# First row tile of tokens in one transfer, and 16 lines of a bias loaded first from ScalarE

## The chip, the cores and the metric

The kernel runs on one core of one Trainium2 chip. The metric is the device time of one execution in microseconds. Each engine of the core (PE for matmuls, with its weight loads as PEld; VectorE, called DVE; ScalarE, called ACT; GpSimd, called POOL; SyncE, called SP) runs its own list of instructions in order, and waits on semaphores for the others and for transfers.

## The reference, cut to what matters

```python
def _A_ref(x, wqkv, wo):                      # x 1 x 2048 x 448, 16 heads of 28
    qkv = (x @ wqkv).reshape(B, S, 3, H, Dh).transpose(2, 0, 3, 1, 4)
    q, k, v = qkv
    idx = pos[:, None] - arange(8) * 2        # eight earlier positions, two apart
    logits = einsum("bhsd,bhswd->bhsw", q, k[idx]) * Dh ** -0.5
    attn = softmax(where(idx >= 0, logits, -1e9))
    return einsum("bhsw,bhswd->bhsd", attn, v[idx]).reshape(B, S, D) @ wo

def _B_ref(x, w1, b1, w2, b2):                # hidden width 1792
    h = relu(x @ w1 + b1)
    return (h * h) @ w2 + b2

g = sigmoid((x * gate_w).sum(-1, keepdims=True))
out = g * _A_ref(x, wqkv, wo) + (1 - g) * _B_ref(x, w1, b1, w2, b2)
```

All data are float32.

## The kernel before

Every matmul is done in three products of a reduced float32 type: each operand is split into a high part (a cast on ScalarE, or on VectorE) and a low part (the difference, on VectorE), and high times high, high times low and low times high are summed in PSUM. The 2048 tokens are four column blocks `c` of 512, held transposed: `xT[c]` has 128 partitions, and 4 row tiles `k` of the width 448, three of 128 rows and a last one of 64 rows that stands twice. "First row tile of tokens" is `xT[0, :, 0]`: 128 lines of 512 numbers, 256 KB.

The program first multiplies all four blocks with the weights of q, k and v (`qkv`), then runs the hidden layer (`h`, `b`) with the attention on GpSimd and VectorE beside it, and last the projection (`a`). A planner written in Python lays out the order of each engine's instructions: it keeps a clock of PE's work, and `when(t, ...)` and `at(dt, ...)` put a load or a split into the program when that clock comes to `t`.

The opening is written out by hand. PE runs 13 warm-up matmuls on a tile of zeros (line 634, tile `zero`, line 631). SP issues for each `k` a transfer of the weights of q (`raws[0]`, `wqraw` in the profile) and then the tokens (`rx`, `xraw`); for `k` = 0 the tokens come in two transfers of 256 columns. Each is split as soon as it is there: line 657 makes the weights' high part on ScalarE, lines 662 and 664 the tokens' high part in two halves of 256 columns (for the very first half on VectorE, line 662), lines 665 and 667 the low parts on VectorE:

```python
        for i, cols in enumerate(halves):
            if k == i == 0:
                nc.vector.tensor_copy(x.h[k][:, cols], rx[:, k, cols])
            else:
                nc.scalar.activation(x.h[k][:, cols], rx[:, k, cols], AF.Copy)
```

`qkv_first` (line 255) then does the first 36 matmuls, 12 for each of three row tiles: for `k` = 0 first those of token groups 0 and 1 (columns 0 to 255), then those of groups 2 and 3. The matmuls of the fourth row tile and all later ones are issued in pairs on the two halves of PE's rows (line 186).

`b1z` is a small tile: columns 0 to 13 hold the first bias (`b1t`, 128 lines of 14 numbers, 56 bytes), and one number in column 15 of partition 0 is a zero (`none`, set in line 632). `biases()` loads `b1` and `b2` from SP when the planner's clock is at 70 us. All loads are issued by SP. The load of the tokens of block 1 (`x_load`, line 561) is four transfers, one for each row tile.

Of the kernel before, what the change touches and what calls it, by code (L numbers as in the profile page):

```python
# [14 lines left out]
P = 128  # L15
# [7 lines left out]
CH = 512  # L23
# [34 lines left out]
def gated_mix_kernel(ctx: ExitStack, tc: tile.TileContext, xT, wqkv, w1, w2, wo, b1, b2, out):  # L58
    nc = tc.nc
# [43 lines left out]
    b1t, none = b1z[:, :NF], b1z[0:1, 15:16]  # L103

    ctx.enter_context(tc.manual_schedule())
    nc.gpsimd.memset(mask, 0.0)
    for s in range(HALO):
        nc.gpsimd.memset(mask[0:1, s, 0:HALO - s], -1e9)
# [388 lines left out]
    def raw_tile(name):  # L497
        return rawp.tile([P, 4, 512], F32, tag="raw", name=name)
# [62 lines left out]
    def x_load(c):  # L561
        raw = raw_tile(f"xraw{c}")
        if c == 1:
            for k in range(4):
                nc.sync.dma_start(raw[:, k, :CH], xT[c, :, k])
        else:
            nc.sync.dma_start(raw[:, :, :CH], xT[c])
        return raw
# [69 lines left out]
    rx = raw_tile("xraw0")  # L638
    for k in range(4):
        if k < 3:  # L640
            nc.sync.dma_start(raws[0][:, k, :NQ], wqkv[0, :, k])
        else:
            for b, rows in ((0, slice(0, 64)), (1, slice(64, P))):
                nc.sync.dma_start(raws[0][rows, k, :NQ], wqkv[b, rows, k])
        for cols in ((slice(0, 256), slice(256, CH)) if k == 0 else (slice(0, CH),)):
            nc.sync.dma_start(rx[:, k, cols], xT[0, :, k, cols])

    for b, tag in ((1, "k"), (2, "v")):
        raw = attp.tile([P, 3, D], F32, tag=tag, name=f"wqraw{b}")
# [67 lines left out]

    xs, xm = {0: x}, {}
    xraw = {1: x_load(1)}
    SPLIT_AT = {1: 19000.0, 2: 35000.0, 3: 53500.0}  # L720

# [16 lines left out]
    def x_more(c):  # L738
        xraw[c] = x_load(c)
# [3 lines left out]
            nc.sync.dma_start(d.rearrange("a g r c -> (a g) r c")[:, 0:HALO], halo0)  # L743

    def biases():
        nc.sync.dma_start(b1t, b1)
        nc.sync.dma_start(b2t, b2.partition_broadcast(P))

    for k in range(3):
# [22 lines left out]
    when(67000.0, w1_piece, 2, 77400.0, 1450.0)  # L772
    when(68000.0, w1_piece, 3, 83300.0, 1450.0)
    when(70000.0, biases)
    when(86000.0, w2_piece, 0, 4, 93000.0, 1400.0)
    when(89600.0, w2_piece, 4, 3, 100200.0, 1400.0)
# [312 lines left out]
    c, x = ORDER[0], xm[3]  # L1089
# [8 lines left out]
    for g in range(2, 2 * NF):  # L1098
        i, f = g // (NF // 2), g % (NF // 2) * 2
        c = ORDER[i]  # L1100
# [120 lines left out]
```

## Time and profile before

| | us |
|---|---|
| median of 3 runs | 413.23 (413.23 to 413.26) |
| profiled execution | 413.8 |
| its span | 412.0 |
| PE busy | 407.8 (99%) |
| DVE busy | 270.6 (66%) |
| POOL busy | 268.4 (65%) |
| ACT busy | 210.4 (51%) |

The profile is of one execution. Its span counts from the first instruction of the program to the last; the rest of its own time lies around it. In the views, a row of the timeline gives the start and the length in us, the engine, the line of the kernel, the operation, the tile written and the tiles read, the shape, and how many; in brackets stands how long the engine was idle before it, and what ended that. SPq is the queue that issues transfers: the length of its row is the time of issuing, not of the transfer. In the rows of busy time by stretch stand the stretch, its length, the busy time of PE, PEld, DVE, ACT and POOL with the instructions in it, the clock granted to PE, the share of the DMA engines, and GB/s.

### The profile page before, as it was taken

The page shows a single profiled execution, that of the slowest core. Times are in us where ns is not written, and L with a number is a line of the kernel's source. Part 1 is how long each engine was busy: PE and PEld are TensorE (multiplying, and loading weights), DVE is VectorE, ACT ScalarE, POOL GpSimd, SP SyncE. Part 2 cuts the span into 40 slices and gives each one's busy share as a digit, 9 for nine tenths or more (in the row PEclk, how much of TensorE's full clock was granted, in tenths as well). Part 3 has the DMA queues.
Part 4 walks back from the last instruction along what each step waited for, and adds up shares of the span by engine and source line. Part 5 has one row for each costly group of instructions (what it writes and reads, how often), then busy time and mean ns, then how long its engine had stood idle before and what let it go on. Part 6 is the DMA issues. An engine that isn't in the chain of part 4 may idle for free.

```text
span 412.0 us, 9331 instructions
## 1 busy us (share of the span) xinstructions
PE 407.8 (99%) x3835; PEld 366.0 (89%) x3835; DVE 270.6 (66%) x430; ACT 210.4 (51%) x461; POOL 268.4 (65%) x167
## 2 busy tenths in 40 slices
PE   8999999999999999999999999999999999999997
PEld 7999999999888888888888888989898888888996
DVE  4590745276767766787656798879576677892354
ACT  4641646387775555444565535444653254346540
POOL 0000001955999999989989899999899977940000
PEclk9999999999999999999999999999999999999999
DMA  7999999979262315654112649765146530168304
GB/s 213 368 351 309 286 390 288 355 223 315 91 241 99 128 51 209 208 186 152 41 47 105 222 158 270 196 146 154 28 157 200 217 130 2 45 179 132 95 0 181
DMA packets 66763, 73.83 MB, mean 179 GB/s; under 512 B 33120, under 2 KB 59296, under 8 KB 66464
## 3 DMA queue, kind: packets, MB, share of 16 engines
q1 hardware_dynamic: 66720, 73.23, 55.4%
q8 instruction: 30, 0.49, 0.5%
q14 instruction: 13, 0.11, 0.1%
HBM read 45.74 MB, written 28.28 MB: 180 GB/s over the span
## 4 chain that ended last, share of the span: by engine, by line
PE 99%; DVE 0%; issue 0%
PE b L186 33%; PE h L186 32%; PE qkv L186 23%; PE a L186 7%; PE qkv L255 2%; PE warm L634 1%; PE a L993 1%; PE last L993 0%; DVE bt L872 0%; PE last L985 0%; PE a L985 0%; DVE zero L631 0%; DVE b1z L632 0%
## 5 line engine op out<-in xcount | busy, mean ns | idle before, releaser
L335 POOL TENSOR_TENSOR qk<-q,k 128x896 f32<-128x896 f32 x64 | 135.2, 2144 | 84.2 <-DMA k<-k_d 76.0
L342 POOL TENSOR_TENSOR av<-lg,v 128x896 f32<-128x896 f32 x64 | 119.2, 1957 | 6.2 <-DVE lg L336 5.6
L621 DVE TENSOR_TENSOR h<-h,h 128x512 fp32r<-128x512 f32 x56 | 38.4, 688 | 66.8 <-ACT h L624 66.5
L186 PE MATMUL qkv<-wqh,x 64*128 64x448 f32 x528 | 78.2, 359 | 0.0
L336 DVE TENSOR_REDUCE lg<-qk 128x32 f32<-128x896 f32 x64 | 67.0, 1074 | 0.0
L350 DVE TENSOR_REDUCE o<-av 128x112 f32<-128x896 f32 x64 | 66.4, 1070 | 0.1
L186 PE MATMUL b<-w2ah,h 64*128 64x448 f32 x448 | 66.3, 359 | 0.0
L186 PE MATMUL b<-w2bh,h 64*128 64x448 f32 x448 | 66.1, 359 | 0.0
L622 ACT ACTIVATE h<-h,b1z 128x512 f32<-128x512 f32 x56 | 36.7, 655 | 43.6 <-PE h L186 43.6
L186 PEld LDWEIGHTS qkv<-wqh,x 64*128 64x128 f32 x528 | 49.4, 184 | 3.6
L186 PE MATMUL qkv<-wql,x 64*128 64x448 f32 x264 | 47.7, 358 | 0.0
L186 PEld LDWEIGHTS b<-w2bh,h 64*128 64x128 f32 x448 | 42.1, 184 | 3.5
L186 PEld LDWEIGHTS b<-w2ah,h 64*128 64x128 f32 x448 | 42.0, 184 | 3.7
L205 ACT ACTIVATE st<-qkv 128x448 f32<-128x448 f32 x48 | 23.5, 542 | 34.3 <-PE qkv L186 31.7
L186 PE MATMUL b<-w2bl,h 64*128 64x448 f32 x224 | 40.7, 358 | 0.0
L186 PE MATMUL b<-w2al,h 64*128 64x448 f32 x224 | 40.5, 358 | 0.0
L623 ACT ACTIVATE h<-h 128x512 fp32r<-128x512 f32 x56 | 33.5, 598 | 1.7
L624 ACT ACTIVATE h<-h 128x512 f32<-128x512 f32 x56 | 33.3, 594 | 0.0
L573 ACT ACTIVATE h<-h 128x4 fp32r<-128x4 f32 (+1 forms) x35 | 7.2, 207 | 44.4 <-PE b L186 44.2
L186 PE MATMUL h<-x2b,w1h 64*128 64x512 f32 x168 | 28.1, 386 | 0.0
L186 PE MATMUL h<-x,w1h 64*128 64x512 f32 x168 | 28.1, 386 | 0.0
L186 PE MATMUL h<-x1b,w1h 64*128 64x512 f32 x168 | 28.1, 386 | 0.0
(150 smaller groups left out, 688.6 us busy)
## 6 DMA issues: line engine op xcount, KB each, us to landing
k<-k_d SPq DMA_DIRECT2D x8, 840.0 KB, 5.6
v<-v_d SPq DMA_DIRECT2D x8, 840.0 KB, 5.0
x_d<-x SPq DMA_DIRECT2D x11, 512.0 KB, 6.8
q_d<-st SPq DMA_DIRECT2D x8, 448.0 KB, 5.5
k_d<-st SPq DMA_DIRECT2D x8, 448.0 KB, 5.2
v_d<-st SPq DMA_DIRECT2D x8, 448.0 KB, 5.8
w1raw<-w SPq DMA_DIRECT2D x4, 896.0 KB, 9.2
q<-q_d SPq DMA_DIRECT2D x8, 448.0 KB, 3.6
```

Source lines behind the costliest of these rows:

```text
L186: nc.tensor.matmul(acc.pt[:, :acc.n], a[rows], w[rows], start=acc.todo == acc.all, stop=acc.todo == 1)
L205: nc.scalar.activation(st[:, :, t % 2], pt[:, :D].rearrange("p (g c) -> p g c", g=G), AF.Copy)
L255: nc.tensor.matmul(acc.pt[:, :D], a, w, start=k == j == 0, stop=False)
L335: nc.gpsimd.tensor_mul(pr, q[:, s:s + 1].to_broadcast([P, W, C]), k[:, s:s + W])
L336: pending.append(lambda: nc.vector.tensor_reduce(lg[:, s], pr.rearrange("p w (h d) -> p w h d", h=HG), axis=AX.X, op=ALU.add))
L342: nc.gpsimd.tensor_mul(pr.rearrange("p (h d) w -> p w h d", h=HG), lg[:, s][:, :, :, None].to_broadcast([P, W, HG, DH]), v[:, s:s + W].rea ...
L350: nc.vector.tensor_reduce(o[:, g * C:(g + 1) * C], pr, axis=AX.X, op=ALU.add)
L573: nc.scalar.activation(ap, f32(ap), AF.Copy)
L621: nc.vector.tensor_sub(hl, pt, f32(hh))
L622: ops += [lambda pt=pt, r=r: nc.scalar.activation(pt, pt, AF.Relu, bias=b1t[:, f + r:f + r + 1]), lambda pt=pt, hh=hh: nc.scalar.activatio ...
L623: lambda pt=pt, hh=hh: nc.scalar.activation(hh, pt, AF.Square),
L624: lambda pt=pt, r=r, low=low: (nc.scalar.activation(pt, pt, AF.Square), at(delays[r], low))]
```

## The change

ScalarE issues, as its first instruction, the transfer of lines 0 to 15 of the first bias; the later load from SP brings lines 16 to 127. The tokens of block 0, row tile 0, come in one transfer of 512 columns instead of two of 256; their splits stay in halves. In `x_load` the four transfers of block 1 are written with slices of length one and are the same transfers.

```diff
     ctx.enter_context(tc.manual_schedule())
+    nc.scalar.dma_start(b1t[0:16], b1[0:16])
     nc.gpsimd.memset(mask, 0.0)
...
         if c == 1:
-            for k in range(4):
-                nc.sync.dma_start(raw[:, k, :CH], xT[c, :, k])
+            for ks in [slice(k, k + 1) for k in range(4)]:
+                nc.sync.dma_start(raw[:, ks, :CH], xT[c, :, ks])
...
-        for cols in ((slice(0, 256), slice(256, CH)) if k == 0 else (slice(0, CH),)):
-            nc.sync.dma_start(rx[:, k, cols], xT[0, :, k, cols])
+        nc.sync.dma_start(rx[:, k], xT[0, :, k])
...
     def biases():
-        nc.sync.dma_start(b1t, b1)
+        nc.sync.dma_start(b1t[16:P], b1[16:P])
         nc.sync.dma_start(b2t, b2.partition_broadcast(P))
```

## The prediction

> **What bounds the kernel now.** I read the page first, then the chain of waits, then the timeline of the first 14 us, because the change touches only what is loaded there.
>
> ```profile
> span 412.0 us, 9331 instructions
> PE 407.8 (99%) x3835; PEld 366.0 (89%) x3835; DVE 270.6 (66%) x430; ACT 210.4 (51%) x461; POOL 268.4 (65%) x167
> ...
> PE 99%; DVE 0%; issue 0%
> ```
> ```profile
> 4.34 8.87 PE qkv L255 x36
> 13.21 91.55 PE qkv L186 x912
> 104.76 2.77 PE h L186 x24
> ```
>
> PE is busy 99% of the span and carries 99% of the chain. The second fence is the chain in order of time (start, length, what). The 912 matmuls from 13.21 run as pairs on two row halves, 456 pairs in 91.55 us, 0.2 us a pair. There is no hole in that, so what shifts the start of this stream shifts the end by as much: nothing later can absorb it. The question is the 36 matmuls of line 255 before it, which need the first row tile of tokens. The timeline of their stretch (start, length, engine, line, what; in brackets the idle time before it and what ended it):
>
> ```profile
> 0.74 1.28 ACT L657 ACT_TABLE_LOAD   x1 [0.74 <-PEq L1213]
> 0.75 0.39 SPq L641 DMA_DIRECT2D wqraw<-wqkv  x1
> 1.08 0.06 DVE L632 MEMSET b1z<- 1x1 f32 x1
> 1.19 3.14 PE L634 MATMUL warm<-zero 128*128 128x256 f32 x13 [1.19 <-DVE b1z L632]
> 1.19 0.89 SPq L646 DMA_DIRECT2D xraw<-xT  x2
> 2.13 0.43 SPq L641 DMA_DIRECT2D wqraw<-wqkv  x1
> 2.60 0.43 SPq L646 DMA_DIRECT2D xraw<-xT  x1
> 3.45 0.58 ACT L657 ACTIVATE wqh<-wqraw 128x448 fp32r<-128x448 f32 x1 [1.43 <-DMA wqraw<-wqkv]
> 3.79 0.29 DVE L662 CAST x<-xraw 128x256 fp32r<-128x256 f32 x1 [2.65 <-DMA xraw<-xT]
> 4.06 0.62 DVE L665 TENSOR_TENSOR wql<-wqraw,wqh 128x448 fp32r<-128x448 f32 x1
> 4.22 1.09 PE L255 MATMUL qkv<-wqh,x 128*128 128x448 f32 x2
> 5.62 0.42 ACT L664 ACTIVATE x<-xraw 128x256 fp32r<-128x256 f32 x1 [1.59 <-DMA xraw<-xT]
> 7.66 0.72 ACT L664 ACTIVATE x<-xraw 128x256 fp32r<-128x256 f32 x2 [0.84 <-DMA xraw<-xT]
> 8.64 0.57 PE L255 MATMUL qkv<-wql,x 128*128 128x448 f32 x2
> 9.05 0.96 PE L255 MATMUL qkv<-wqh,x 128*128 128x448 f32 x4
> 9.84 0.56 PE L255 MATMUL qkv<-wql,x 128*128 128x448 f32 x2
> 12.65 0.56 PE L255 MATMUL qkv<-wqh,x 128*128 128x448 f32 x2
> 13.14 0.47 PE L186 MATMUL qkv<-w7h,x 64*128 64x448 f32 x2
> ```
>
> Two things are to be seen. First, the split of the tile works as a relay. The first half is used at 3.79, the second only at 5.62, and PE begins at 4.22 on the first half alone, when the 13 warm-up matmuls have just run out. Second, PE has two paces. Here PE alone, the same stretch:
>
> ```profile
> 4.74 0.57 PE L255 MATMUL qkv<-wqh,x 128*128 128x448 f32 x1
> 5.11 0.95 PE L255 MATMUL qkv<-wql,x 128*128 128x448 f32 x2
> 5.86 1.59 PE L255 MATMUL qkv<-wqh,x 128*128 128x448 f32 x4
> 7.29 0.56 PE L255 MATMUL qkv<-wql,x 128*128 128x448 f32 x2
> 7.68 1.12 PE L255 MATMUL qkv<-wqh,x 128*128 128x448 f32 x4
> ```
>
> From 4.74 to 5.86 three matmuls start, 0.373 us each; from 8.64 to 9.84 six, 0.20 us each, of the same shape. The pace changes between the fourth start after 5.86 and 7.29, about 7.2. So PE ran at half pace for 6.0 us from its first warm-up matmul at 1.19, working almost without a hole, and only then at full pace. In the half-pace stretch PE itself is the bound: the second half, usable from 6.04 (5.62 and 0.42), arrived before PE asked for it. The last start at 12.65 is the first of two, so the 36 end their slots at 13.05.
>
> **The change part by part.**
>
> *The tile in one transfer.* SP's issue slots are 0.47 us apart (2.13 to 2.60). One slot goes, so the second weight block and the second token tile are issued one slot earlier. But the first half no longer comes alone. When does the whole tile land? The transfers' sizes and the rates:
>
> ```profile
> wqraw<-wqkv SPq DMA_DIRECT2D x3, 225.0 KB, 4.1
> ot<-o_d SPq DMA_DIRECT2D x16, 32.0 KB, 2.4
> xraw<-xT SPq DMA_DIRECT2D x2, 128.0 KB, 3.3
> b1z<-b SPq DMA_DIRECT2D x1, 7.0 KB, 8.6
> 0.00:2.00 2.00, 0.81 (x3) 0.81 (x4) 0.27 (x2) 1.26 (x1) 0.80 (x13) 1.00 0.15 25
> 2.00:4.00 2.00, 2.00 (x11) 2.00 (x10) 0.21 (x1) 0.57 (x2) 0.00 (x0) 1.00 0.68 196
> 2.50:2.75 0.25, 0.25 (x3) 0.25 (x3) 0.00 (x0) 0.00 (x0) 0.00 (x0) 1.00 1.04 368
> 4.00:4.25 0.25, 0.25 (x3) 0.10 (x2) 0.25 (x2) 0.03 (x1) 0.00 (x0) 1.00 0.80 203
> ```
>
> (DMA issues: size, us to landing; then busy time by stretch, whose last two columns are the DMA share and GB/s. The row 2.50:2.75 is the best rate of the start.) The earliest: the first half was there at 3.79, and another 128 KB at 368 GB/s is 0.35 us, so 4.14. The latest: 5.62, when the second half was used. Between them: weights and tile are 225 + 256 = 481 KB; the stretches had moved 50 + 392 = 442 KB by 4.00 and 51 more by 4.25. All 481 KB were therefore on the way by about 4.2. At the mean rate of 2.00:4.00 the 225 KB of the weights were moved by about 2.9 and used at 3.45, the 353 KB with the first half by 3.55 and used at 3.79; a lag of 0.25 to 0.55 gives 4.4 to 4.8, and the issue slot saved takes back up to 0.47. I take 4.4, nearer the early end, because bytes and order are the same and one issue is saved.
>
> From the tile to PE: cast, semaphore and weight load took 3.79 to 4.22 = 0.43 us. So the first real matmul comes at 4.83 instead of 4.22; the weights' high part (3.45 + 0.58 = 4.03) is early enough. The low part of the weights now stands behind the cast on VectorE, until 4.40 + 0.29 + 0.62 = 5.31, and it is wanted by the third matmul, two half-pace slots after 4.83, at 5.58: no wait. ScalarE's half of the cast runs beside it (0.42 us).
>
> PE thus has a hole of 0.6 us where it had almost none. What it costs depends on the pace. Unhurt, the pace rises at 7.2 as before: (7.2 - 4.83) / 0.373 = 6.4 matmuls, the other 29.6 at 0.2 us are 5.9 us, end 13.13, or +0.1 us. Set back fully, the 6.0 us of half pace begin anew at 4.83 and end at 10.83: 16.1 matmuls by then, 19.9 at 0.2 us are 4.0 us, end 14.8, or +1.75 us. The trace of before has no hole in the warm-up, so these are the two bounds. I take the second: 3.0 us of work before 4.2 were not enough for full pace and 6.0 us without a hole were, and now the stretch has a hole in its middle.
>
> *The rule for this, weighed.*
>
> ```profile
> 0.37:3.78 3.41, 2.59 (x12) 2.59 (x13) 0.27 (x2) 1.61 (x2) 0.67 (x12) 1.00 0.46 120
> 3.78:7.20 3.42, 3.42 (x11) 2.96 (x11) 2.01 (x5) 1.24 (x3) 0.00 (x0) 1.00 0.93 268
> ```
>
> PE was busy 2.59 of the 3.41 us before 3.78 and stayed at half pace; it was busy in all of the next 3.42 us, and the full pace followed. The Trainium skill ("TensorE: Matmul & The Clock Gate", section "Part 1: The HAM clock gate") says that the clock is halved until one free-running window of about 3.4 us was busy; the trace agrees if 76% is too little, and by that rule the next chance after 7.20 is 10.61, an estimate that makes the sum +1.7 us.
>
> *The 16 lines from ScalarE.* One issue before ScalarE's table load, 0.4 us like SP's rows. ScalarE idles 1.43 us before 3.45, which hides it; without that cover it would cost its 0.4 us. On the DMA engines it is 16 of 128 lines of a 7 KB transfer, ahead of or beside the first weights. Its cost for the loads lies between nothing (a gain, if it takes a first-access delay off the weights, has no row) and one slot of 0.47; I take 0.1, in which the weights' path (4.03) still stays behind the tile's.
>
> *The rest of the bias* keeps SP's place with 112 lines. Its reader is the Relu after the matmuls that start at 104.76, far behind an 8.6 us landing. The four loads of row tile 1 are the same transfers. Both at nothing.
>
> The profiled execution took 413.8 for its span of 412.0; the runs' median is 413.23, so I add +1.75 to the median: 415.0. A difference of 0.2%, 0.83 us, is about what a measurement of this kernel can tell from no change.
>
> **The rivals.**
>
> *The pace rises at 7.2 all the same* (the hole is too short to matter). By the sum above 413.3; with the tile at 4.14 it is 413.1; with the tile at 5.62, first matmul 6.05, 3.1 matmuls before 7.2 and 32.9 after it: 13.78, +0.7, so 414.0. For it: the hole is a tenth of the 6.0 us. Against: nothing in the trace shows full pace after a broken stretch. This is the not slower side, and it decides at a hole somewhere between the 0.1 us of now and the 0.82 us (3.41 - 2.59) that were too much before 3.78.
>
> *Faster: the loads come earlier and PE can use it.* Today the second token tile is used at 7.66, the only wait for data in the 36. If it comes 0.47 us earlier and the pace were full before 7.2, the later 24 matmuls start 0.5 us earlier: 412.7; if the slow first transfers gain still more, up to twice that, 412.2. Against: PE's half pace, not the data, holds the first 12.
>
> *The memset of line 632 waits for the 16 lines.* It writes another column of the same tile `b1z`, and the profile puts the start of the warm-up down to it. Should it wait for the landing, issue at 0.75 and 2.4 us as for the smallest landing quoted, the warm-up begins at 3.2, and the first real matmul 3.03 us after it as now (1.19 to 4.22), at 6.2; full pace comes 6.0 us after 3.2, at 9.2: 8.0 of the 36 by then, 28.0 at 0.2 us after it, the end is 14.8, so 415.0 in another way. Against: the columns don't overlap, and the warm-up itself reads only `zero`.
>
> *No effect at all* is not likely as a case of its own, since the first matmul cannot start before the whole tile is there.
>
> The Trainium skill ("DMA: Bandwidth & Descriptors", section "Rules for kernel authors") advises to coalesce small transfers; by it alone the tile would come at the early end and the sum be 413.1. The trace shows the price that it leaves out: a half that is used 1.8 us before the other.
>
> **How the numbers follow.** Forecast (hole, pace set back) 0.52, nearly all over 0.2%, 0.02 of it for a shorter setback; pace unhurt 0.27, all within; memset 0.10, of which 0.02 within; faster 0.11, of which 0.02 within. Slower 0.58, same 0.33, faster 0.09. The forecast's own range is 414.5 (tile at 4.14, first matmul 4.57, +1.5 less a little) to 416.2 (tile at 5.62: +3.0); a tile later than 5.0 I hold for less than 1 in 10, so the range ends at 415.6. Below it reaches over the unhurt case with a little of the faster one, to 412.9. It leaves out some 0.16.
>
> **What would show it.** Right: the first matmul of line 255 near 4.8, a hole in PE after the warm-up, 0.37 us pace until about 10.8, the stream of line 186 from about 14.9 and 0.2 us a pair after it. Wrong: 0.2 us pace from 7.2 (the setback fails), a tile used before 4.2 or after 5.2 (the landing), a warm-up that begins later than 1.2 (the memset), or a line 186 that starts before 13.1.

## The result, and the profile after

The changed kernel takes 415.91 us (median of 6 runs, 414.36 to 416.85) against 413.23 before: ratio 1.0059, interval 1.0044 to 1.0075, so 2.7 us slower by the medians. It also spreads: 2.5 us between its fastest and slowest run, where those of before lay within 0.8 us (412.6 to 413.4; of its 36 runs beside the experiments below, 35 lie between 412.86 and 413.7 and one at 415.42). The profiled execution took 415.37, its span is 413.6. The page, and the chain of waits in order of time:

```profile
span 413.6 us, 9330 instructions
PE 407.7 (99%) x3835; PEld 366.0 (88%) x3835; DVE 270.4 (65%) x430; ACT 210.5 (51%) x461; POOL 268.5 (65%) x167
...
PE 98%; DMA 1%; DVE 0%; ACT 0%; SPq 0%; issue 0%
```
```profile
1.20 4.36 DMA xraw<-xT
6.02 8.77 PE qkv L256 x36
14.79 91.53 PE qkv L187 x912
```

PE's work is what it was (407.7 us), and the stream of 912 matmuls runs as before (91.53 us). It begins 1.6 us later, and the chain now starts with a transfer: the first token tile. (In the changed kernel the lines ahead of the token loads are one higher: 256 is the old 255, 187 the old 186; those behind, such as 657 and 662, are the same.) The timeline of the changed kernel, and PE alone:

```profile
0.74 0.42 ACTq L106 DMA_DIRECT2D b1z<-b  x1
1.20 0.42 SPq L646 DMA_DIRECT2D xraw<-xT  x1
1.66 0.43 SPq L642 DMA_DIRECT2D wqraw<-wqkv  x1
1.20 3.15 PE L635 MATMUL warm<-zero 128*128 128x256 f32 x13 [1.20 <-DVE b1z L633]
3.34 0.58 ACT L657 ACTIVATE wqh<-wqraw 128x448 fp32r<-128x448 f32 x1 [0.86 <-DMA wqraw<-wqkv]
5.58 0.29 DVE L662 CAST x<-xraw 128x256 fp32r<-128x256 f32 x1 [4.44 <-DMA xraw<-xT]
7.75 0.72 ACT L664 ACTIVATE x<-xraw 128x256 fp32r<-128x256 f32 x2 [1.01 <-DMA xraw<-xT]
```
```profile
6.02 1.09 PE L256 MATMUL qkv<-wqh,x 128*128 128x448 f32 x2 [1.68 <-ACT x L664]
6.90 0.95 PE L256 MATMUL qkv<-wql,x 128*128 128x448 f32 x2
7.65 1.54 PE L256 MATMUL qkv<-wqh,x 128*128 128x448 f32 x4
9.02 0.56 PE L256 MATMUL qkv<-wql,x 128*128 128x448 f32 x2
9.43 0.96 PE L256 MATMUL qkv<-wqh,x 128*128 128x448 f32 x4
14.71 0.48 PE L187 MATMUL qkv<-w7h,x 64*128 64x448 f32 x2
```

The whole tile is used at 5.58, as late as its second half was before (5.62), though it was issued as early as the first half. PE has a hole of 1.7 us, then starts at 6.02, at half pace (two matmuls start between 6.90 and 7.65, 0.375 us each) until about 8.9, and at 0.2 us a matmul from 9.02 on. Where did the tile's time go? Busy time by stretch, the last two columns again DMA share and GB/s:

```profile
3.00:3.50 0.50, 0.50 (x5) 0.50 (x3) 0.00 (x0) 0.16 (x1) 0.00 (x0) 1.00 0.93 233
3.50:4.00 0.50, 0.50 (x4) 0.50 (x3) 0.00 (x0) 0.41 (x1) 0.00 (x0) 1.00 0.91 71
4.00:4.50 0.50, 0.34 (x2) 0.04 (x1) 0.00 (x0) 0.00 (x0) 0.00 (x0) 1.00 0.64 93
4.50:5.00 0.50, 0.00 (x0) 0.00 (x0) 0.00 (x0) 0.00 (x0) 0.00 (x0) 1.00 0.41 134
5.00:5.50 0.50, 0.00 (x0) 0.00 (x0) 0.00 (x0) 0.00 (x0) 0.00 (x0) 1.00 0.80 307
```

From 3.5 to 5.0 the transfers crawl at 71 to 134 GB/s, with several queued. The kernel before has such a stretch from 3.25 to 4.0 as well (73 to 148 GB/s); the first half of its tile was in use at 3.79 all the same.

The column of the granted clock reads 1.00 in all these rows, at half pace too. The trace's record of the clock begins with its first change, the grant of the full clock (8.88 us in the changed kernel, 7.20 before), and the view counts the time ahead of it as full. At the start of the program the pace must therefore be read from the starts of the matmuls, or from that first entry.

### The profile page after: what moved, and what is told of

Its sections match the earlier page's. It is cut to its first block, busy times and chain, and to the rows that moved or that the text cites. A ratio compares the mean times of both kernels' runs of the same rounds, so it can differ in the third digit from the quotient of the medians.

```text
span 413.6 us, 9330 instructions
## 1 busy us (share of the span) xinstructions
PE 407.7 (99%) x3835; PEld 366.0 (88%) x3835; DVE 270.4 (65%) x430; ACT 210.5 (51%) x461; POOL 268.5 (65%) x167
## 4 chain that ended last, share of the span: by engine, by line
PE 98%; DMA 1%; DVE 0%; ACT 0%; SPq 0%; issue 0%
PE b L187 33%; PE h L187 32%; PE qkv L187 23%; PE a L187 7%; PE qkv L256 2%; DMA xraw<-xT 1%; PE a L993 1%; PE last L993 0%; DVE bt L872 0%; ACT x L664 0%; SPq L642 0%; PE last L985 0%; PE a L985 0%
## 5 line engine op out<-in xcount | busy, mean ns | idle before, releaser
L187 PE MATMUL h<-x0b,w1h 64*128 64x512 f32 x168 | 28.1, 386 | 0.0
```

What stands on the lines that cost most here:

```text
L187: nc.tensor.matmul(acc.pt[:, :acc.n], a[rows], w[rows], start=acc.todo == acc.all, stop=acc.todo == 1)
```

## The experiments

Theory A: the tile comes late, and the hole that this leaves behind PE's warm-up puts the full pace off; each costs for itself. Rivals: the transfer from ScalarE has a part in it; the late tile alone costs, and the pace has nothing to do with PE's hole. Beside the first four kernels the kernel before took 413.3.

**The halves back, ScalarE's transfer kept** (`e1_halves`).

```diff
-        nc.sync.dma_start(rx[:, k], xT[0, :, k])
+        for cols in ((slice(0, 256), slice(256, CH)) if k == 0 else (slice(0, CH),)):
+            nc.sync.dma_start(rx[:, k, cols], xT[0, :, k, cols])
```

> The changed kernel with the first token tile in two halves again; the 16 lines from ScalarE stay. If the late tile is the cause (A), the first real matmul is back near 4.2 us and the time near 413.2. If the transfer from ScalarE has a part of its own (B), some of the loss stays: first matmul 4.3 to 4.7, time 413.4 to 414.5.

413.26 us, ratio 0.9999 (0.9991 to 1.0008). ScalarE's transfer costs nothing that can be measured, and the first real matmul is back at 4.23:

```profile
4.23 0.78 PE L256 MATMUL qkv<-wqh,x 128*128 128x448 f32 x2
4.86 0.57 PE L256 MATMUL qkv<-wql,x 128*128 128x448 f32 x2
```

In this execution full pace is there by 4.86 (0.2 us a matmul; the clock record has the grant at 4.53), although the warm-up is that of the kernel before, whose profiled execution ran at half pace until 7.2.

**One transfer alone, nothing from ScalarE** (`e2_one`): the kernel before with the inverse of that edit.

> The kernel before with the first token tile in one transfer, and nothing else of the change. A: the whole loss, tile used near 5.6 us, time 415.9 within 0.6. B (ScalarE's transfer takes a part): the tile is used by 5.2 and the time is 414 to 415.

415.79 us (414.63 to 417.54), ratio 1.0063 (1.0042 to 1.0084): the whole loss. The profiled execution happened to be the shortest of them, 414.63, and shows the late tile with an unhurt pace:

```profile
5.50 0.29 DVE L661 CAST x<-xraw 128x256 fp32r<-128x256 f32 x1 [4.36 <-DMA xraw<-xT]
5.94 0.64 PE L255 MATMUL qkv<-wqh,x 128*128 128x448 f32 x2 [1.60 <-ACT x L663]
6.90 0.97 PE L255 MATMUL qkv<-wqh,x 128*128 128x448 f32 x4
13.91 0.48 PE L186 MATMUL qkv<-w7h,x 64*128 64x448 f32 x2
```

Nearly the same hole as in the changed kernel, but 0.24 us a matmul from 5.94 and 0.2 from 6.90 on. The full clock was granted at 4.71, inside the hole. The longest run of the same program is 2.9 us over this one; that it had half pace where this one has not is likely, but it has no trace.

**The hole filled, the tile as late** (`e3_warm22`): the changed kernel.

```diff
-WARM = 13
+WARM = 22
```

> The changed kernel with 22 warm-up matmuls instead of 13, so that PE works until the tile is there. A (a hole sets the clock back): the first real matmul stays near 6.0, but full pace comes between 4.2 and 8.0; (8.0 - 6.0) / 0.373 = 5.4 matmuls at half pace at worst, so the time is 413.4 to 414.3. B (the loss is the late tile alone, and the pace follows PE's start or nothing at all): as the changed kernel, near 415.9.

414.54 us, four of five runs within 414.47 to 414.55 (the fifth 415.35), ratio 1.0032 (1.0020 to 1.0044). Above the time that was expected, but about half of the loss is gone, and most of the spread:

```profile
1.20 4.83 PE L635 MATMUL warm<-zero 128*128 128x256 f32 x22 [1.20 <-DVE b1z L633]
5.69 0.29 DVE L662 CAST x<-xraw 128x256 fp32r<-128x256 f32 x1 [4.55 <-DMA xraw<-xT]
6.13 0.64 PE L256 MATMUL qkv<-wqh,x 128*128 128x448 f32 x2
7.08 0.96 PE L256 MATMUL qkv<-wqh,x 128*128 128x448 f32 x4
8.29 1.17 PE L256 MATMUL qkv<-wqh,x 128*128 128x448 f32 x4
13.79 0.47 PE L187 MATMUL qkv<-w7h,x 64*128 64x448 f32 x2
```

No hole, and full pace at once: 0.24 us a matmul from 6.13 to 7.08, 0.2 after it (the full clock was granted at 5.61, within the 4.2 to 8.0 that were expected). What is left, 1.2 us, is the late tile alone, with a small wait for the second tile at 8.29 (1.17 for four instead of 0.96), which my expectation had not counted.

**The hole without a late tile** (`e4_warm7`): the kernel before with `WARM = 7`.

> The kernel before with 7 warm-up matmuls instead of 13: a hole of about 1.3 us before 4.2, and the data as early as before. A (a hole sets the clock back): the first matmul stays at 4.2, full pace comes between 7.0 and 10.4, the time is 413.2 to 414.6, in the middle 413.9, and it varies from run to run. B (only late data cost): no change, 413.2.

414.5 us (413.7 to 414.75), 1.2 us more by the medians; ratio 1.0020 (1.0007 to 1.0034), which is 0.8 us (0.3 to 1.4). The hole is 1.06 us long, not the 1.3 that were expected.

```profile
1.20 1.86 PE L634 MATMUL warm<-zero 128*128 128x256 f32 x7 [1.20 <-DVE b1z L632]
3.68 0.29 DVE L662 CAST x<-xraw 128x256 fp32r<-128x256 f32 x1 [2.54 <-DMA xraw<-xT]
4.12 1.09 PE L255 MATMUL qkv<-wqh,x 128*128 128x448 f32 x2 [1.06 <-ACT wqh L657]
7.25 0.95 PE L255 MATMUL qkv<-wql,x 128*128 128x448 f32 x2
8.99 0.56 PE L255 MATMUL qkv<-wql,x 128*128 128x448 f32 x2
13.48 0.48 PE L186 MATMUL qkv<-w7h,x 64*128 64x448 f32 x2
```

The data are there as before, the first matmul starts at 4.12, and still half pace lasts until about 8.4 (7.25 and 0.95 for two is half pace, 8.99 and 0.56 full). By the medians this hole alone costs 1.2 us, the late tile alone 1.2 us, and the changed kernel, with a longer hole of 1.7 us, loses 2.7 us: theory A. Which part is the larger the intervals can't tell.

The next four kernels ask why the tile is late; all put it in one transfer on the kernel before (413.43 beside them).

**The tile ahead of the weights** (`f1_tile_first`): its transfer is issued first, the weights' second.

> The kernel before with the first token tile in one transfer, issued ahead of the first weights instead of behind them. Theory A (all loads crawl from about 3.2 to 4.7 us, and what was not landed by then is late): the tile is there by 3.6, the weights' high part starts only at 5.3 to 5.8, and the time is near 415.5. Theory B (a transfer of 256 KB in lines of 2 KB lands late by itself): tile near 5.0, weights by 4.5, time 414.5 to 415.5.

416.47 us, 1.0074 (1.0052 to 1.0095). The weights came late as theory A has it, but the tile and the time fit neither theory.

```profile
4.59 0.29 DVE L664 CAST x<-xraw 128x256 fp32r<-128x256 f32 x1 [3.45 <-DMA xraw<-xT]
5.47 0.58 ACT L659 ACTIVATE wqh<-wqraw 128x448 fp32r<-128x448 f32 x1 [3.44 <-DMA wqraw<-wqkv]
```

Even at the head of the queue the tile is used at 4.59, where the weights in that place are used at 3.2 to 3.5. The transfer in second place is late again (5.47), whatever it carries. Half pace lasted until 12.16 in this execution, 6.1 us after its first real matmul at 6.09.

**Nothing issued behind the tile until it is there** (`f3_hold`).

```diff
+        if k == 0:
+            hold_d = tc.dram_tile([P, 16], F32, name="hold_d")
+            nc.sync.dma_start(hold_d, rx[:, 0, :16])
```

> The kernel before with the tile in one transfer, and behind it on SP a small store that reads the tile, so that no later load is issued before the tile is there. Theory C (the later loads crowd the tile): the tile is there by 4.2, first matmul by 4.7; the second weights come 2 to 3 us after it, so the time is still over 414. Theory A (a slow stretch whatever is queued): the tile is used at 5.3 to 5.7 again, time 416 to 418.

415.73 us, 1.0063 (1.0046 to 1.0080), with the first matmul at 4.70 and the other loads late, as expected. The tile, and its stretch:

```profile
4.26 0.29 DVE L664 CAST x<-xraw 128x256 fp32r<-128x256 f32 x1 [3.12 <-DMA xraw<-xT]
3.00:3.50 0.50, 0.50 (x5) 0.50 (x3) 0.00 (x0) 0.26 (x1) 0.00 (x0) 1.00 0.75 287
3.50:4.00 0.50, 0.50 (x4) 0.50 (x3) 0.00 (x0) 0.32 (x1) 0.00 (x0) 1.00 0.27 98
```

The same two transfers, issued at the same times, are used at 4.26 instead of 5.50 when nothing follows them. A trace keeps every packet of the transfers, here one line each, with its size and its time. By these records all 128 lines of the tile had landed by 3.95 here; in the changed kernel 95 had by 4.0, and the last came at about 5.2. In these single profiles the later loads make up the 1.2 us.

**The tile from ScalarE beside the weights from SP** (`f4_act_tile`): `nc.scalar` instead of `nc.sync` for that transfer.

> The kernel before with the first token tile in one transfer issued by ScalarE, at the same time as SP issues the weights. Theory A (what has not landed by 3.2 us is late; both transfers are then under way together): weights and tile both land after 3.2, one of them or both near 5, time 414.5 to 416. Rival (the place behind the weights in SP's queue was the matter): both are there by 4.2, first matmul by 4.7, time 413.0 to 413.6.

415.89 us, 1.0063 (1.0045 to 1.0081).

```profile
5.33 0.58 ACT L656 ACTIVATE wqh<-wqraw 128x448 fp32r<-128x448 f32 x1 [2.87 <-DMA wqraw<-wqkv]
5.51 0.29 DVE L661 CAST x<-xraw 128x256 fp32r<-128x256 f32 x1 [4.36 <-DMA xraw<-xT]
```

Both are late, as theory A expected: the weights are used at 5.33, the tile at 5.51. A second queue doesn't help here.

**All loads later** (`f5_later`): three transfers of 16 short lines ahead of them on SP.

> The kernel before with the tile in one transfer, and three transfers of 16 short lines ahead of all loads on SP, which put every load about 1.3 us later. If the slow stretch lies at a fixed time of the execution (3.2 to 4.7 us): the weights are used only near 5 and the tile near 5.7 to 6.2. If it comes a fixed time or amount after the loads begin: weights near 4.7, tile near 6.9.

417.74 us, 1.0104 (1.0083 to 1.0126). The first load was issued at 2.66, 1.9 us later than before (not 1.3), the weights were used at 5.49 and the tile at 7.64, both about 2.1 us later than in `e2_one`. The lateness goes with the loads, not with a fixed time of the execution.

```profile
7.64 0.29 DVE L664 CAST x<-xraw 128x256 fp32r<-128x256 f32 x1 [6.50 <-DMA xraw<-xT]
8.08 1.09 PE L255 MATMUL qkv<-wqh,x 128*128 128x448 f32 x2 [3.75 <-ACT x L666]
8.97 0.95 PE L255 MATMUL qkv<-wql,x 128*128 128x448 f32 x2
11.56 0.97 PE L255 MATMUL qkv<-wqh,x 128*128 128x448 f32 x4
16.86 0.48 PE L186 MATMUL qkv<-w7h,x 64*128 64x448 f32 x2
```

With a hole of 3.75 us this is the only trace in which the clock went back before the program's end. Busy time and granted clock by stretch:

```profile
0.84:4.25 3.41, 3.06 (x13) 2.85 (x13) 0.27 (x2) 1.18 (x1) 0.49 (x9) 1.00 0.14 11
4.25:7.66 3.41, 0.09 (x1) 0.00 (x0) 0.02 (x1) 0.59 (x2) 0.00 (x0) 1.00 0.78 214
7.66:11.08 3.42, 3.00 (x8) 2.72 (x9) 2.16 (x6) 1.53 (x4) 0.00 (x0) 0.50 1.06 318
```

The full clock was granted at 4.25, taken back at 7.66 after 3.41 us with 0.09 us of work, and granted again at 11.08.

**Two milder forms of the hold.** `g1_hold_weights` holds the later loads only until the weights have landed, with 16 warm-up matmuls; it is an attempt at a version with one transfer that keeps up. `g2_one_behind` lets one load pass behind the tile and holds the rest.

> The kernel before with the tile in one transfer, a small store behind it on SP that reads the first weights (so that later loads are issued from their landing, about 3.3, on), and 16 warm-up matmuls instead of 13. Theory C (later loads crowd the tile): tile used by 4.4, first matmul by 4.9, no hole over 0.3 us; the second token tile is used near 7.9, so the time is 413.3 to 414.2. If instead the slow stretch comes whatever is behind: tile near 5.5, time 414.5 to 416.

> The kernel before with the tile in one transfer, the second weights behind it, and only then the small store that reads the tile and holds back all other loads. C, if one transfer behind is crowd enough: tile used at 5.2 to 5.7. C, if it takes several: tile used by 4.5. Time over 414.5 in both, since the rest is late.

414.65 us, 1.0033 (1.0020 to 1.0045), and 415.57 us, 1.0054 (1.0034 to 1.0075). In both the tile is used at 4.82, between the 4.26 of nothing behind it and the 5.50 to 5.69 of all loads. For `g1_hold_weights` this misses the 4.4 that crowding had promised: only the small store (at 3.33) was issued before 3.71 there, and some packets of the tile that began from 3.15 on already took 0.6 to 0.8 us, where none took over 0.11 in `f3_hold`. So the order is by what follows, but a few hundred nanoseconds came without any load behind; whether the small store made them is not shown. What in the DMA path slows down, a row of single profiles cannot say; that stays open. No version beat the kernel before.

## Why the prediction was right or wrong

**Right: the bound and the path.** The stream of line 186 passes every delay on to the end. In each of the six profiles whose first row of that stream stands above, the execution's own time less that start is the same within 0.2 us: 415.37 - 14.71 = 400.66 for the changed kernel, 400.72 for `e2_one` (414.63), 400.68 for `e3_warm22` (414.47), 400.63 for `e4_warm7` (414.11), 400.83 for `f5_later` (417.69), and 400.66 before (413.8 - 13.14).

**Right: the step from the tile to the first matmul.** 0.43 us were forecast and 0.44 measured (5.58 to 6.02).

**Wrong: when the tile lands.** Of the bounds 4.14 and 5.62 I took 4.4, since "bytes and order are the same and one issue is saved". It was 5.58, past the 5.2 that I had named as the sign of a wrong landing, and 5.50 and 5.69 in two more kernels. The step that failed is "All 481 KB were therefore on the way by about 4.2": I counted every byte that had moved as one of the weights and the tile, and even so there was no slack: 481 KB of 1024 bytes are 493 thousand bytes, just the 442 and 51 of the stretches. The packet records of the trace before show otherwise: by 4.25, 208 of the tile's 256 half lines had landed, beside 18 lines of the second weights, and the last half line came at 5.29. `f3_hold` (4.26) is near what my rate gives with two transfers alone; with the loads behind them it is 1.2 us more. The late bound was a row for the same bytes at the same place in the queue, and it was the one to take: the forecast's own sum for it is 416.2, beside 415.91 measured. Instead I held a tile later than 5.0 for less than 1 in 10, and that ended the range at 415.6. The Trainium skill ("DMA: Bandwidth & Descriptors", section "Rules for kernel authors") advises to coalesce many small transfers; the early tile that the forecast drew from it did not come: 5.58 for the whole, 3.79 for the first half.

**Right in direction, wrong in form: the setback.** `e4_warm7` shows full pace put off without a late tile, `e3_warm22` a late tile without it. But no fixed 6.0 us of half pace begin at the first real matmul. From there to the full clock it took 2.9 us in the changed kernel (6.02 to 8.88), 4.3 in `e4_warm7`, 6.1 in `f1_tile_first`, and nothing in `e2_one` and `f4_act_tile`, where the grant came inside the hole (4.71 and 4.53). Nor did PE need 6.0 us without a hole: in `e1_halves` it took 3.3 (1.20 to 4.53). The clock records show what stands in its place. In every trace the full clock, once it stays, lasts 118, 119 or 120 times 3.4133 us (406.186 us before, 119 times). In all twelve the 3.41 us right before a grant hold at least 2.77 us of PE work (2.77 in `g2_one_behind`, 2.86 in the changed kernel), and each earlier stretch of that grid, ahead of the first grant, at most 2.76 (`g1_hold_weights`; 2.29 in the changed kernel, 2.05 to 5.46). So a hole can spoil one stretch and put the grant off to the end of a later one, and whether it does depends on where the grid lies, which differs from execution to execution. The Trainium skill ("TensorE: Matmul & The Clock Gate", section "Part 1: The HAM clock gate") has the clock judged by windows that run freely; these figures agree with it. The forecast had weighed this, with the grid of one execution (7.20, 10.61).

For the profiled execution, with the tile's true time: (8.9 - 6.02) / 0.375 = 7.7 matmuls at half pace, and 28.3 at 0.2 us end at 14.6, beside the 14.7 at which the stream began. Two terms were off, one too early and one too long, and there they nearly cancelled, by luck: +1.75 us forecast, +1.57 measured.

**Wrong: the base.** I worked the sum out on the profiled execution of before (413.8, stream from 13.14), and added it to the median (413.23), in which the stream must begin near 12.5 by the 400.7 above (`e1_halves`, profiled at 413.14, has it at 12.37). The profiled execution of before had half pace until 7.2 and was longer than any of the six runs behind the median. That is 0.6 of the 0.9 us by which 415.0 fell short of 415.91; the median run of the changed kernel is another 0.5 us over its profiled one (415.37), and whether by a longer half pace or a later tile no trace shows.

**The rivals.** Pace unhurt at 413.3 (its 413.1 for a tile at 4.14 works out to 413.2): wrong as a forecast of the median, and even the unhurt execution of `e2_one` (414.63) was slower, because of the tile. Memset of line 632 behind the 16 lines: no, the warm-up starts at 1.20 as before. Faster: no; the second token tile came at 7.75 beside 7.66.

## What to carry to other kernels

A first load that is split can be worth more than its bytes say when the consumer can start on a part: here the first half was in use at 3.79, the whole at 5.50 to 5.69, and the split was worth 2.5 us. Let warm-up work last until the first real work, with a margin for the latest landing: a hole of 1.06 us behind it cost 1.2 us here. How long half pace lasts in one profile is no constant to build a sum on; it was 2.9 us in one execution here and 6.1 in another. Before a difference from a profile is added to a median, look where the profiled execution stands among the runs.

## What was not expected of the hardware

In the changed kernel transfers fell to 71 to 134 GB/s for 1.5 us, from 3.5 us on, with more loads queued, and one and the same tile was used at 4.26, 4.82 or 5.50 to 5.69 us depending on what followed it. And after a hole of 1.6 us PE went on at full pace in one execution (`e2_one`) and needed 2.9 us more at half pace in another (the changed kernel). The clock was granted only after 2.77 us of work in 3.41 (81%), but it stayed full through 1.98 us (58%) in `f4_act_tile` (4.53 to 7.94).
